# Gathering a unit's attention products into one block on TensorE, beside the MLP's second product

## The chip, the cores and the metric

The kernel runs on one core of a Trainium2 chip. The metric is the device time of one execution in microseconds (us). TensorE is called PE in the profile, VectorE DVE, ScalarE ACT, GpSimd POOL, and SyncE, which issues most DMAs here, SP.

## The reference

Two blocks follow each other. The first is a gated recurrence over 4 batches x 8 heads, 768 tokens, head size 48; the second is an MLP of 384 -> 2048 -> 384 with ELU over the 3072 tokens.

```python
f = 1.0 / (1.0 + np.exp(-f_logit))
state = np.zeros((B, H, D, D), dtype=np.float32)
for t in range(S):
    state = f[:, :, t, :, None] * state + np.einsum('bhd,bhe->bhde', k[:, :, t], v[:, :, t])
    y[:, :, t] = np.einsum('bhd,bhde->bhe', q[:, :, t], state)
# (B,H,S,D) -> (B*S, H*D)
x = np.ascontiguousarray(y.transpose(0, 2, 1, 3)).reshape(B * S, H * D)
h = x @ w_in
g = np.where(h > 0.0, h, np.exp(np.minimum(h, 0.0)) - 1.0)
out = g @ w_out
```

## The kernel before

**Units and steps.** The function `fast` does the work. Tokens are cut into 12 units of 256 tokens (three a batch), and a unit into four chunks of 64 for the recurrence. The MLP's 2048 hidden features are taken in 8 pairs of 256. The main loop (at the end of `fast`) has 12 x 16 steps, T = 0 to 191; unit m has steps 16m to 16m + 15. An even step issues `up(P)`, the first product of one pair of features (L918; for units from 1 on `up7`, L872: ten products of 128x128 tiles, done with seven multiplications in place of eight, "psH" in the profile, L882). An odd step issues `joined(P)` before anything else (L901: three DVE additions and, through `exped`, two ACT activations, L914 and L915) and at its end `down(P - 2)`, the second product of the pair before the last (L950, "psM", L981; seven products), which sums into four PSUM banks m0 to m3 over the unit's eight pairs. So unit m's last `down` is in step 3 of unit m + 1; it also issues the evacuation of the four banks: one ACT copy (L992), five DVE additions (L991) and four stores. Inside `up7`, after the first four products, DVE makes the first addition out of the bank (L891) and `elu` of the pair before (L936), whose sums POOL then makes (L946).

**The order is written by hand.** Instructions go into each engine's queue in the order of the calls. `at_step(T, ...)` puts calls into `plan`; the main loop runs those of step T after `joined` and before `up` or `down`.

**Attention of a unit** is made of these calls, in this order of data:

- `load` (L431): f, k, q, v by DMA on SP into one of two sets of buffers (unit number modulo 2). `gates` (L607): two ACT activations on f.
- `decays(u, p)` for three pairs of heads (L640): a scan and a reciprocal on DVE (L626, L631), products of k and of the q of the pair before on POOL (L621), and after the third a DMA `move` that fills the fourth pair (L633, "f<-f"). `settle` (L655) makes the rest on POOL.
- `transposed` (L662): eight transposes of k on PE into banks a0, a1 ("psT"), copied by ACT.
- `advance` (L718): 64 products of 64x64 tiles into a0, a1 ("psU"), then `step` four times on DVE (L677), which adds up the states.
- `scores` (L694): 64 such products into a0, a1 ("psS"), and `mask`, two DVE products (L713) into the one buffer "at".
- `outputs` (L734): 64 such products into a0, a1 ("psY", L743), and at its end two ACT copies of a few columns into "between" (L750), which stand between these products and the next ones in the same banks.
- `carried` (L752): up to 64 such products onto the same sums ("psY", L763), three ACT copies to xt and two small DMAs. `blend` (L865) prepares xt for the first product on POOL.

From unit 3 on the steps are given by D3 and A3, counted from t = 16 (u - 1), one unit before the unit's own MLP: `load` at t - 16, `gates` at t - 8, `decays` and `settle` at t - 7, -5, -3, -1, `transposed` at t + 2, `advance` at 4, `step` at 5, `scores` at 7, `outputs` at 9, `carried` at 11, `blend` at 13. So the four blocks of 64x64 tiles lie between the MLP's 128x128 products, each alone. `reread` and `check` (L590, L597) read the weights again by DMA and take their smallest and largest values with two DVE reductions (L603), every fourth step from 48 on, the reductions four steps later.

[...]

## Time and profile before

| What | Value |
|---|---|
| Median of 3 runs | 569.24 us (569.01 to 570.13) |
| Span of the profiled execution | 567.3 us |
| Mean granted TensorE clock | 0.997 |
| PE busy, steady units, 256.85 to 388.17 us | 131.32 of 131.32 us |
| DVE, ACT, POOL busy in the same stretch | 97.09, 50.54, 70.11 us |
| DMA share, GB/s in it | 0.33, 88 to 90 |
| One block: psU, psS, psY (L743), psY (L763) | 64 products of 64x64 tiles each |

The page gives the span of one profiled execution, and no other time for it. Its sections are read in this order: busy time of each engine; the span in 40 slices, with the granted clock and the DMA's share; the chain of work that ended last, by engine and line; the costliest groups with their mean duration and the idle time before them. The chain can also be had in order of time, and the timeline shows instructions merged by line: start in us, duration in us, engine, line, operation, tiles written and read, shape, count, and in brackets the idle time before it with what ended it. The ends of matmuls are modelled, so distances of starts are used for TensorE.

DVE's busy tenths in the 40 slices are 8779989785675785885785885786776876745543: 8 or 9 in places up to slice 8, and 5 to 8 after that.

### The profile page before, as it was taken

The page shows a single profiled execution, that of the slowest core. Times are in us where ns is not written, and L with a number is a line of the kernel's source. Part 1 is how long each engine was busy: PE and PEld are TensorE (multiplying, and loading weights), DVE is VectorE, ACT ScalarE, POOL GpSimd, SP SyncE. Part 2 cuts the span into 40 slices and gives each one's busy share as a digit, 9 for nine tenths or more (in the row PEclk, how much of TensorE's full clock was granted, in tenths as well). Part 3 has the DMA queues.
Part 4 walks back from the last instruction along what each step waited for, and adds up shares of the span by engine and source line. Part 5 has one row for each costly group of instructions (what it writes and reads, how often), then busy time and mean ns, then how long its engine had stood idle before and what let it go on. Part 6 is the DMA issues. An engine that isn't in the chain of part 4 may idle for free.

```text
span 567.3 us, 15527 instructions
## 1 busy us (share of the span) xinstructions
PE 547.5 (97%) x6336; PEld 509.7 (90%) x6336; DVE 409.4 (72%) x802; ACT 230.2 (41%) x424; POOL 292.7 (52%) x567
## 2 busy tenths in 40 slices
PE   6879998999999999999999999999999999999996
PEld 3566677999999999999999999999999999999996
DVE  8779989785675785885785885786776876745543
ACT  3287862443343433434343343333343343233331
POOL 6601788475374465456366357257248348325332
PEclk9899999999999999999999999999999999999999
DMA  8997951024024225215216216206206203201001
GB/s 212 266 261 209 298 129 43 3 47 114 3 46 138 65 52 145 79 42 156 78 36 155 86 38 153 86 19 173 84 14 178 84 6 74 84 2 36 29 2 35
DMA packets 38193, 53.30 MB, mean 94 GB/s; under 512 B 3712, under 2 KB 27936, under 8 KB 38112
## 3 DMA queue, kind: packets, MB, share of 16 engines
q1 hardware_dynamic: 37312, 51.62, 34.2%
q8 instruction: 52, 0.85, 0.7%
q10 hardware_dynamic: 800, 0.59, 0.4%
q14 instruction: 29, 0.24, 0.1%
HBM read 44.04 MB, written 4.72 MB: 86 GB/s over the span
## 4 chain that ended last, share of the span: by engine, by line
PE 81%; DMA 7%; DVE 7%; issue 2%; POOL 1%; ACT 1%; SPq 0%; DVEq 0%; ACTq 0%; POOLq 0%
PE psH L882 36%; PE psM L981 36%; DMA area<-in_moe_w_in_dram 4%; PE psS L705 2%; PE psY L743 2%; PE psY L763 2%; PE psU_a L728 2%; DVE f L631 2%; PE psT L669 1%; DMA xt<-xt 1%; DMA f<-f 1%; DVE f L626 1%; DMA k<-in_k_dram 1%; DVE bits L563 1%; DVE area L850 1%
## 5 line engine op out<-in xcount | busy, mean ns | idle before, releaser
L882 PE MATMUL psH<-xt,wi 128*128 128x128 f32 (+1 forms) x1056 | 195.0, 294 | 0.1
L946 POOL TENSOR_TENSOR sums<-gg 128x128 f32<-128x128 f32 x176 | 77.7, 462 | 214.5 <-DVE gg L936 205.9
L882 PEld LDWEIGHTS psH<-xt,wi 128*128 128x128 f32 x1056 | 149.5, 192 | 1.8 <-DVE hh L891 0.4
L914 ACT ACTIVATE gg<-hh 128x512 f32<-128x512 f32 x88 | 55.5, 631 | 232.0 <-DVE hh L904 154.6
L882 PE MATMUL psH<-xt,area 128*128 128x128 f32 x704 | 121.8, 275 | 1.3 <-DVE hh L904 1.0
L882 PEld LDWEIGHTS psH<-xt,area 128*128 128x128 f32 x704 | 106.5, 191 | 6.3 <-PE psH L882 1.3
L891 DVE TENSOR_TENSOR hh<-psH,u 128x256 f32<-128x256 f32 x88 | 37.1, 422 | 93.9 <-ACT u L889 93.9
L981 PE MATMUL psM<-area,sums 128*128 128x192 f32 x528 | 100.2, 326 | 0.0
L981 PEld LDWEIGHTS psM<-area,sums 128*128 128x128 f32 x528 | 88.2, 190 | 0.0
L981 PE MATMUL psM<-wo,gg 128*128 128x192 f32 x352 | 74.9, 335 | 0.0
L631 DVE RECIPROCAL f<-f 128x256 f32<-128x256 f32 x36 | 62.7, 1747 | 1.1
L936 DVE SCALAR_TENSOR_TENSOR gg<-gg,hh 128x512 f32<-128x512 f32 x88 | 61.9, 703 | 1.5 <-ACT gg L915 1.5
L915 ACT ACTIVATE gg<-gg 128x512 f32<-128x512 f32 x96 | 60.6, 631 | 3.0
L981 PEld LDWEIGHTS psM<-wo,gg 128*128 128x128 f32 x352 | 55.2, 190 | 2.0
L904 DVE TENSOR_TENSOR hh<-psH,u43h 128x256 f32<-128x256 f32 (+1 forms) x176 | 54.7, 352 | 3.0
L946 POOL TENSOR_TENSOR sums<-gg,sums 128x128 f32<-128x128 f32 x88 | 47.0, 534 | 6.9
L889 ACT COPY u<-psH 128x128 f32<-128x128 f32 x88 | 23.1, 263 | 60.9 <-PE psH L882 60.9
L621 POOL TENSOR_TENSOR q<-q,f 128x256 f32<-128x256 f32 x48 | 35.7, 745 | 21.8 <-DVE f L631 10.6
L904 DVE TENSOR_TENSOR u43h<-psH,hh 128x256 f32<-128x256 f32 x88 | 37.1, 422 | 12.7 <-PE psH L882 12.4
L621 POOL TENSOR_TENSOR k<-k,f 128x256 f32<-128x256 f32 x48 | 40.7, 851 | 7.1 <-DMA f<-f 5.1
L981 PE MATMUL psM<-area,gg 128*128 128x192 f32 x176 | 43.0, 326 | 0.0
L981 PE MATMUL psM<-wo,sums 128*128 128x192 f32 x176 | 43.0, 326 | 0.0
(97 smaller groups left out, 672.3 us busy)
## 6 DMA issues: line engine op xcount, KB each, us to landing
area<-in_moe_w_out_dram SPq DMA_DIRECT2D x8, 768.0 KB, 9.6
again<-in_moe_w_in_dram SPq DMA_DIRECT2D x16, 384.0 KB, 4.2
again<-in_moe_w_out_dram SPq DMA_DIRECT2D x16, 384.0 KB, 3.5
k<-in_k_dram SPq DMA_DIRECT2D x12, 384.0 KB, 4.5
q<-in_q_dram SPq DMA_DIRECT2D x12, 384.0 KB, 5.4
v<-in_v_dram SPq DMA_DIRECT2D x12, 384.0 KB, 5.8
area<-in_moe_w_in_dram SPq DMA_DIRECT2D x8, 576.0 KB, 8.4
out_dram<-o SPq DMA_DIRECT2D x42, 96.0 KB, 1.7
```

The lines of the kernel that those rows point to most:

```text
L621: e.tensor_tensor(out=t[n][:, p], in0=t[n][:, p], in1=t["f"][:, p, "kq".index(n)], op=ALU.mult)
L631: nc.vector.reciprocal(f[:, p, 1], f[:, p, 0])
L705: nc.tensor.matmul(pc[r][FULL[b], w, p], lhsT=t["k"][FULL[r], p, cols], rhs=t["q"][FULL[r], p, cols], start=True, stop=True,)
L882: nc.tensor.matmul(to, lhsT=lhs, rhs=rhs, start=(n == 0), stop=True, skip_group_check=True)
L889: nc.scalar.copy(u1[:], pa[:, 0])
L891: add = lambda to, x, y: nc.vector.tensor_tensor(out=to, in0=x, in1=y, op=ALU.add)
L904: add = lambda to, x, y: nc.vector.tensor_tensor(out=to, in0=x, in1=y, op=ALU.add)
L914: nc.scalar.activation(g[:], h, AF.Relu, scale=-1.0)
L915: nc.scalar.activation(g[:], g[:], AF.Exp, scale=-1.0)
L936: nc.vector.scalar_tensor_tensor(out=g[:], in0=g[:], scalar=-1.0, in1=phs.pop(P), op0=ALU.add, op1=ALU.max)
L946: nc.gpsimd.tensor_tensor(out=s[:, i], in0=x, in1=y, op=op)
L981: nc.tensor.matmul(pm[bank][:, half * DH : (half + 1) * DH], lhsT=x, rhs=y, start=first, stop=(j == NP - 1), skip_group_check=True,)
```

## The change

Up to unit 4 the attention is still planned call by call (unit 3 in the steps it had; unit 4 now at 29 to 48, earlier by 3 to 8 steps). From unit 5 on, everything comes a unit earlier (t = 16 (u - 2)), and the products are issued together in `turn(u)` at t + 5: `outputs` of unit u - 1, `scores` and `mask` of unit u, `carried` of unit u - 1, `advance` and the four `step` of unit u. Scores go to m3 and m0 and the states' products to m1 and m2, the banks of the second product of unit u - 3, whose last `down` is in step t + 3; outputs and carried keep a0 and a1. The `down` of step t + 5 isn't issued there: step t + 7 issues two, one after the other. So turns are at steps 53, 69, ... 149. Outputs and carried of the last unit stand alone at 165 and 167. `load` is split in two (f and k; q and v), and the rereading of the weights moves by two steps.

```diff
--- before.py
+++ after.py
@@ -401,9 +401,17 @@
     D2 = (16, 18, 20, 22)
     A2 = (23, 25, 25, 26, 27, 28)
     D3 = (-7, -5, -3, -1)
-    A3 = (2, 4, 5, 7, 9, 11)
+    FIRST = 4
+    BEFORE = (
+        (16, 16, 24, (25, 27, 29, 31), (34, 36, 37, 39, 41, 43)),
+        (29, 29, 32, (33, 35, 37, 40), (44, 46, 46, 48)),
+    )
+    SECOND = (40, 43, 42)
+    DS = (-4, -2, 0, 1)
+    TR = 2
+    TURN = 5
     BL = 13
-    RR = 0
+    RR = 2
     MX = 10
     CB = 16
     BL1 = 13
@@ -715,10 +723,10 @@
                 in1=twice[:].unsqueeze(1).broadcast_to([128, NW * HP, C]), op=ALU.mult,
             )
 
-    def advance(u, pairs=range(HP)):
+    def advance(u, pairs=range(HP), banks=("a0", "a1")):
 
         if u not in pus:
-            pus[u] = [ps.tile([128, NW, HP, D], FP32, tag=n, name=f"psU{u}_{n}") for n in ("a0", "a1")]
+            pus[u] = [ps.tile([128, NW, HP, D], FP32, tag=n, name=f"psU{u}_{n}") for n in banks]
         pu = pus[u]
         for p in pairs:
             for w in range(NW):
@@ -829,13 +837,29 @@
         kept = []
         for p, i in enumerate(first):
             at_step(i, (lambda: settle(u)) if p == NKT else lambda p=p: decays(u, p))
+        if not then:
+            return
         if u > 1:
             at_step(then[0], lambda: transposed(u, 0, "a0"), lambda: transposed(u, 1, "a1"))
         at_step(then[1], lambda: advance(u))
         at_step(then[2], *(lambda c=c: step(u, c) for c in range(NC)))
         at_step(then[3], lambda: kept.append(scores(u)), lambda: mask(u, kept[0]))
-        at_step(then[4], lambda: outputs(u))
-        at_step(then[5], lambda: carried(u))
+        if len(then) > 4:
+            at_step(then[4], lambda: outputs(u))
+            at_step(then[5], lambda: carried(u))
+
+    def turn(u):
+
+        if u > FIRST:
+            outputs(u - 1)
+        if u < NU:
+            mask(u, scores(u, ("m3", "m0")))
+        if u > FIRST:
+            carried(u - 1)
+        if u < NU:
+            advance(u, banks=("m1", "m2"))
+            for c in range(NC):
+                step(u, c)
 
     gs, ss, pms, phs = {}, {}, {}, {}
 
@@ -1132,11 +1156,22 @@
     at_step(BL1, lambda: blend(1))
     at_step(30, lambda: blend(2))
     for u in range(3, NU):
-        t = (u - 1) * NFT
-        at_step(t + BL, lambda u=u: blend(u))
-        at_step(t - 16, lambda u=u: load(u))
-        at_step(t - 8, lambda u=u: gates(u))
-        attention(u, [t + i for i in D3], [t + i for i in A3])
+        at_step((u - 1) * NFT + BL, lambda u=u: blend(u))
+        if u <= FIRST:
+            fk, qv, gate, first, then = BEFORE[u - 3]
+            attention(u, first, then)
+        else:
+            t = (u - 2) * NFT
+            fk, qv, gate = (t - 15, t - 10, t - 9) if u > FIRST + 1 else SECOND
+            attention(u, [t + i for i in (D3 if u > FIRST + 1 else DS)], ())
+            at_step(t + TR, lambda u=u: transposed(u, 0, "a0"), lambda u=u: transposed(u, 1, "a1"))
+            at_step(t + TURN, lambda u=u: turn(u))
+        at_step(fk, lambda u=u: load(u, "fk"))
+        at_step(qv, lambda u=u: load(u, "qv"))
+        at_step(gate, lambda u=u: gates(u))
+    at_step((NU - 2) * NFT + TURN, lambda: outputs(NU - 1))
+    at_step((NU - 2) * NFT + TURN + 2, lambda: carried(NU - 1))
+    turns = [(u - 2) * NFT + TURN for u in range(FIRST + 1, NU)]
     for n in range(NR):
         t = 3 * NFT + (NU - 4) * NFT * n // NR + RR
         at_step(t, lambda n=n: reread(n))
@@ -1154,7 +1189,9 @@
             f()
         if T % 2 == 0:
             up(P)
-        elif P >= LAG:
+        elif P >= LAG and T not in turns:
+            if T - 2 in turns:
+                down(P - LAG - 1)
             down(P - LAG)
         for n in later.pop(T, ()):
             split(n)
```

## The prediction

> **What bounds the kernel now.** I read the page first: busy time, chain, costliest groups.

> ```profile
> span 567.3 us, 15527 instructions
> ...
> PE 547.5 (97%) x6336; PEld 509.7 (90%) x6336; DVE 409.4 (72%) x802; ACT 230.2 (41%) x424; POOL 292.7 (52%) x567
> ...
> PE psH L882 36%; PE psM L981 36%; DMA area<-in_moe_w_in_dram 4%; PE psS L705 2%; PE psY L743 2%; PE psY L763 2%; PE psU_a L728 2%; DVE f L631 2%; PE psT L669 1%; DMA xt<-xt 1%; DMA f<-f 1%; DVE f L626 1%; DMA k<-in_k_dram 1%; DVE bits L563 1%; DVE area L850 1%
> ```

> TensorE carries the chain, and the four attention groups are 2% each. A busy PE row alone proves little, so I took the chain in order of time, where each piece starts when the one ahead lets it.

> ```profile
> 322.99 2.44 PE psH L882 x20
> 325.43 1.09 PE psY L743 x64
> 326.52 2.47 PE psM L981 x14
> 328.99 2.44 PE psH L882 x20
> ...
> 335.00 2.44 PE psH L882 x20
> 337.44 2.28 PE psM L981 x14
> 339.71 2.44 PE psH L882 x20
> ```

> Two steps without attention take 339.71 - 335.00 = 4.71 us (I use 4.72 = 2.44 + 2.28). Two steps with one attention block take 328.99 - 322.99 = 6.00 us, so a block costs 1.28 us. A unit has eight such pairs, one set of transposes (8 x 0.11 = 0.87 us) and four blocks: 37.76 + 0.87 + 5.12 = 43.75 us. The timeline has the transposes of neighbouring units at 305.24 and 348.98: 43.74 us. So from about the third unit on TensorE runs without a gap, and a microsecond won or lost there is one of the kernel.

> Now the price of a block's two ends. In the timeline, 64 products of 64x64 tiles start from 325.36 to about 326.31, 15 ns apart: 64 x 15.1 = 0.96 us. The rest of the 1.28 us, 0.32, is the change of tile shape in and out. Next, what ACT does with the outputs block:

> ```profile
> 325.36 1.16 PE L743 MATMUL psY<-at,v 64*64 64x64 f32 x64
> ...
> 326.64 0.63 ACT L914 ACTIVATE gg<-hh 128x512 f32<-128x512 f32 x1 [2.46 <-DVE hh L904]
> 327.30 0.63 ACT L915 ACTIVATE gg<-gg 128x512 f32<-128x512 f32 x1
> 327.84 0.34 ACT L750 COPY between<-psY 128x8 f32<-128x8 f32 x2
> ```

> The small copy "between" (L750) must be done before carried's products may add to the same banks, and stands in ACT's queue behind the step's two activations. It ends 2.8 us after the block began. Here two steps lie between outputs and carried, so nobody waits. Last, the end of a unit, where the change puts its block:

> ```profile
> 311.12 0.30 ACT L992 COPY u<-psM 128x192 f32<-128x192 f32 x1
> ...
> 311.46 0.36 DVE L991 TENSOR_TENSOR o<-psM,u 128x192 f32<-128x192 f32 x1 [1.62 <-ACT u L992]
> 311.92 1.02 DVE L991 TENSOR_TENSOR u<-psM,u 128x192 f32<-128x192 f32 x2
> 312.97 0.82 DVE L991 TENSOR_TENSOR o<-psM,u 128x192 f32<-128x192 f32 x2
> 313.71 1.00 DVE L603 TENSOR_REDUCE spans<-again 128x1 f32<-128x384 f32 x2
> 314.63 0.41 DVE L891 TENSOR_TENSOR hh<-psH,u 128x256 f32<-128x256 f32 x1
> ...
> 316.01 0.62 DVE L904 TENSOR_TENSOR hh<-psH,u43h 128x256 f32<-128x256 f32 x2
> ...
> 316.73 0.63 ACT L914 ACTIVATE gg<-hh 128x512 f32<-128x512 f32 x1 [3.27 <-POOL sums L946]
> ```

> DVE empties the four product banks until 313.79; hh, elu and the joins stand behind that, and the activations behind these.

> [...]

> **The change part by part.** I count from D = 310.83, where the last second-product pair of a unit (start 310.66, pitch 0.16) makes room for the next instruction.

> 1. Fewer changes of shape. Units 4 to 11 have 32 blocks now. After: advance and scores of unit 4 (2), seven turns, outputs and carried of unit 11 (2): 11 runs. 21 x 0.32 = 6.7 us gained, 3 x 0.32 = 0.96 a turn. The products themselves are as many as before.

> 2. The wait in the turn. PE order at step 5 is outputs, scores, carried, advance, and only scores lies between outputs and carried. PE: up of step 4 is done at D + 2.44, outputs start at D + 2.55, outputs and scores take 1.93, so carried is up at D + 4.48. DVE: the evacuation ends at 313.79 = D + 2.96. The checks (L603), which stood next, move by two steps, so hh can start at about D + 2.88 in place of 314.63; from there to the last join the trace shows 316.63 - 314.63 = 2.00, so D + 4.88. ACT: activations 0.1 later, from D + 4.98 and D + 5.64; between starts 0.54 after the second (327.84 - 327.30), D + 6.18, its first copy ends at D + 6.35, carried starts at D + 6.45. The wait is 6.45 - 4.48 = 1.97 us. From below: the step-9 example alone, without the evacuation ahead, gives copy end 2.65 to 2.8 after block start against 1.93, 0.8 us. From above: if hh came only 0.3 us sooner than now, at D + 3.5, 2.6 us. I take 1.97. Net per turn 1.97 - 0.96 = +1.0 us; seven turns +7.1 us. Behind carried on PE stand advance and the next up; DVE's joins and ACT don't wait for these, but PE never gets the time back.

> 3. Banks. Scores needs m3 and m0, released by DVE's first three instructions (by about D + 1.9), before D + 3.5; advance needs m1 and m2, free at D + 2.96. The second product's next group, at step 7, needs mask (0.68 x 2, D + 4.9 to 6.2) and the states (1.84, from about D + 8.6 to 10.5); step 7 comes at about D + 11. Half a microsecond of cover; nothing lost, up to 0.5 a turn if DVE is later.

> 4. The down at step 5 goes to step 7, two in a row: same instructions, 2 x 2.28. Its sums are long done; the rings of gg (4) and sums (3) just suffice: the oldest user of each was read at step 3. Zero. DVE after the turn (states 1.84, check 1.0, hh to join 2.0) ends near D + 13.4; next need is up of step 8 near D + 15.6.

> 5. Loads in two halves, on SP: the same DMAs; q and v wait for carried two units back, at the turn one step earlier. The page gives f 3.6, k 4.5, q 5.4 us to landing; f has six steps (16 us) to its gates, k more, q five (13 us) to its product. The stores and moves that SP queues behind q wait at most for that turn. Zero. For unit 5, f is issued at 40 and used at 42, 6 us for 3.6. Zero, up to 1.

> 6. The packed stretch, steps 29 to 53. Units 4 and 5 make their decays a unit earlier: 3 x (0.75 + 1.75) = 7.5 us of DVE each; between 128 and 184 us the page's slices have DVE at 5, 6, 7 and 5 tenths, so there is room for both on the whole. A late join has about 3.4 us of slack before up needs its bank. One place is short: unit 5's last reciprocal pair is at 48, its settle at 49, its transposes at 50. At 46 DVE has states (1.84, from 1.25 after advance begins) and 2.5 of decays, then 2.0 hh to join, until 7.6; at 48 mask to 8.9, decays to 11.4. POOL then has k, q (0.7 each), sums 1.85, q, k (0.7 + 1.18): to about 16.3. PE reaches the transposes of pair 3 at 12.0 + 0.66. Wait 3.6. The same shape is seen in unit 2, with one step more:

> ```profile
> 97.68 1.17 POOL L621 TENSOR_TENSOR k<-k,f 128x256 f32<-128x256 f32 x1
> ...
> 98.91 0.44 PE L669 MATMUL psT<-ident,k 128*128 128x128 f32 x2 [0.88 <-POOL k L621]
> ```

> There k ends 6.1 us after the reciprocal (92.75), and PE loses 0.9. Bounds 0.5 to 4; I take 3.2, as DVE may win some time.

> Sum: +7.1 + 3.2 = +10.3 us. The profiled span 567.3 becomes 577.6. The page gives no other time for that execution; the span lies 1.9 us under the median, 569.24. I add 1.9: 579.5 us.

> **The rivals.** B, partly hidden: evacuation and joins overlap better than I laid out, the wait in a turn is 0.8 to 1.0 us and eats just what the shape changes give. Then only part 6 is left: 569 to 573, middle 571. For it: the step-9 lines. Against it: the evacuation ahead in the same FIFO. C, the other side: scores covers the copy, because between is done early. The turn then keeps 0.96 x 7 = 6.7, part 6 costs 2, and the time is 564.5 (561 to 568). It decides from a copy that ends at most 1.9 us after the outputs start; the shortest in the trace is 2.8, so it needs a queue order other than the program's. That the change doesn't join the blocks is no other case; it would look like B. D, worse: the gaps bring the clock down. [...] For it: a gap of 2 us after products of small tiles; against it: the granted clock stays at nine tenths or more through the gaps near 95 us.

> **How the numbers follow.** Forecast 0.63 (574 to 584), B 0.15, C 0.08, D 0.14. A measurement of this kernel tells about 0.2%, 1.1 us, from no change. Slower: forecast, D and four fifths of B, 0.88; within: 0.03; faster: C and a bit of B, 0.09. The range drops C and the greater part of D: 569 to 586.

> **What would show it.** Right: in each turn, PE idle of about 2 us ahead of carried's products (L763's successor) with ACT between as releaser, up to seven times; a unit of 44.7 us in place of 43.75; a PE wait of some 3 us on POOL k once, near 180 us; no wait at the second product's first pair. Wrong: carried follows scores at once, units of 42.8 us (C); or scores itself waits on DVE o (D). If units are 43.7 us, B.

## The result, and the profile after

The changed kernel takes 585.46 us (584.74 to 586.2, four runs) against 569.12 us (also four runs by then): ratio 1.030, 95% interval 1.0272 to 1.0329. It is slower by 16.3 us; the forecast was 10.3. Its profiled execution has a span of 584.5 us against 567.3.

Line numbers have moved: first product L906 (was L882), second L1005 (L981), scores L713, advance L736, outputs L751, "between" L758, carried L771. From the page of the changed kernel:

```profile
span 584.5 us, 15570 instructions
...
PE 548.6 (94%) x6336; PEld 513.0 (88%) x6336; DVE 404.0 (69%) x802; ACT 231.5 (40%) x424; POOL 291.5 (50%) x567
...
PE psH L906 33%; PE psM L1005 31%; DVE f L639 3%; PE psY L751 2%; DMA area<-in_moe_w_out_dram 2%; PE psY L771 2%; DVE hh L928 1%; PE psU_m L736 1%; PE psT L677 1%; DMA k<-in_k_dram 1%; DVE u43h L928 1%; ACT gg L938 1%; DMA f<-f 1%; DMA f<-in_f_logit_dram 1%; DVE f L634 1%
```

PE has the same 6336 products and is busy about as long as before, in a span 17 us longer. On balance what came on is waiting; in the busy time fewer shape changes (6.7 us by part 1's estimate) and slower products (three stretches of 3.41 us at half the clock, below) nearly cancel. DVE's join (L928) and ACT's activations (L938) are on the chain now. The chain's pieces in order of time show a turn (start, duration, what):

```profile
235.59 2.44 PE psH L906 x20
238.03 1.16 PE psY L751 x64
...
239.25 0.43 DVE u43h L928
...
239.70 0.63 DVE hh L928 x2
...
240.42 0.64 ACT gg L938
...
241.61 0.16 ACT between L758
...
241.81 1.28 PE psY L771 x61
...
243.16 1.21 PE psU_m L736 x59
244.37 2.64 PE psH L906 x20
247.01 4.55 PE psM L1005 x28
```

It is the path of the forecast, step by step: outputs, and then carried not before join, two activations and the copy. Counted as in the forecast, from D (here 235.43), DVE's hh starts at D + 2.89, the last join ends at D + 4.89 and the copy starts at D + 6.18; the forecast had 2.88, 4.88 and 6.18. The waits table sums it up for PE (total, times, longest):

```profile
PE psY L771 <- ACT between L758: 13.2, 8, 1.9
```

Seven of the eight are the turns; the eighth, 0.7 us, lies in the first 70 us, and the kernel before has it too. In the timeline the gap is 1.73 us in five turns and 1.93 or 1.94 in two. It counts from the modelled end of the last score. From start to start, as the forecast counts, PE stands still for 1.93 to 1.94 us in the five turns and 2.14 in the two; the forecast was 1.97. The two are the turns in which carried belongs to the first unit of a batch: it leaves out the first chunk (240 pairs of weight load and product in the turn in place of 256), so its first products go to the second bank, and wait for the second of the two copies, too.

Distances between the transposes of neighbouring units are 45.14, 44.85, 44.86, 44.85 and 46.40 us, where they were 43.74: three turns cost 1.11 us each, one 1.40, one 2.66. The 0.3 us more in the first of these come from a short stop in advance's products (0.17 us longer than usual from start to start, at 243.35), of a kind that the run with the copy first explains below. In the last one the gap is 1.93 us, as long as in an earlier turn, and half the clock follows. From the windows table (a stretch, its length, busy time and count by engine, then the granted clock):

```profile
241.93:245.34 3.41, 3.41 (x137) 3.26 (x138) 0.05 (x1) 2.09 (x5) 0.00 (x0) 1.00 0.04 8
...
282.89:286.31 3.42, 2.33 (x131) 2.07 (x129) 3.39 (x9) 0.72 (x2) 1.61 (x4) 1.00 0.21 62
286.31:289.72 3.41, 2.56 (x117) 2.51 (x118) 0.71 (x2) 2.16 (x6) 0.12 (x1) 1.00 0.11 34
419.43:422.84 3.41, 1.48 (x88) 1.34 (x83) 1.79 (x4) 1.49 (x5) 1.48 (x4) 1.00 0.21 62
422.84:426.25 3.41, 3.41 (x72) 3.32 (x62) 1.53 (x5) 1.73 (x3) 0.00 (x0) 0.50 0.10 25
```

The trace's clock records show half the clock in this execution for stretches of 3.41 us: from 37.13 (while the kernel starts), 132.71, 183.91 and 422.84 us, and at its very end. The distances of these four are 28, 15 and 70 times 3.413 us, so they lie on one grid of such stretches. The gap ahead of 422.84 lies whole in one stretch of the grid (PE busy for 1.48 of 3.41 us), and the next one has half the clock. The gap of 1.94 us at 285.2 to 287.2 is cut by a boundary of the grid into 1.08 and 0.85, and nothing follows. The clock is 1.00 in the other six turns.

The rest is lost before the first turn, between steps 32 and 52, in three places. Lines from the timeline of the changed kernel; brackets give the idle time before an instruction and what ended it:

```profile
128.12 0.84 ACT L620 ACTIVATE f<-f 128x768 f32<-128x768 f32 x1 [2.67 <-DMA k<-in_k_dram]
...
129.75 0.24 ACT L913 COPY u<-psH 128x128 f32<-128x128 f32 x1
...
130.50 0.49 PE L906 MATMUL psH<-xt,wi 128*128 128x128 f32 x2 [1.09 <-DVE hh L915]
...
132.70 1.48 PE L906 MATMUL psH<-xt,wi 128*128 128x128 f32 x4
...
163.34 0.66 PE L677 MATMUL psT<-ident,k 128*128 128x128 f32 x4 [0.55 <-ACT xt L780]
...
184.04 0.69 PE L677 MATMUL psT<-ident,k 128*128 128x128 f32 x2 [2.67 <-POOL k L629]
```

First, step 32: unit 4's gates stand in ACT's queue and wait 2.67 us for their load. The small copy (L913) that frees the first product's bank stands behind them, DVE's addition behind the copy, and PE waits. Afterwards four products take 1.48 us where 0.82 is usual: the clock is at half. Transposes, up and down of steps 34 and 35 take 2.12 + 4.33 + 3.01 us from start to start in place of 0.87 + 2.44 + 2.28: 3.9 us. Second, step 44: transposes need bank a1, which ACT's copies of carried, issued one step before, still read; with the down ahead, 1.1 us. Third, step 50: pair 3 of unit 5 waits for k, 3.1 us, and the up after it takes 3.78 us, 1.3 too many, for the most part at half the clock. The windows table has the clock, 0.50, in the first and the third:

```profile
132.71:136.12 3.41, 3.41 (x15) 3.23 (x14) 3.21 (x5) 1.81 (x5) 1.69 (x4) 0.50 0.00 0
...
183.91:187.32 3.41, 3.28 (x16) 3.28 (x17) 0.55 (x2) 0.85 (x2) 0.76 (x2) 0.50 0.87 244
```

Sum: 7.4 us in the five turns with a measured distance, about 1.1 each in the first and the last, 3.9 + 1.1 + 4.4 before: 19.0. This execution reached the up of step 30 1.8 us earlier than that of before (118.95 against 120.75), which leaves 17.2, the difference of the spans. These 1.8 us are not the change's: in the runs below the same point lies anywhere from 118.38 to 120.42. The profiled execution is the slowest of the four, with a mean clock of 0.987; the other three have 0.993 to 0.996 and took 0.7 to 1.5 us less. So the sizes of the losses by the clock are those of this execution.

### The profile page after: what moved, and what is told of

It reads as the page before. It is cut to its first block, busy times and chain, and to the rows that moved or that the text cites. A ratio compares the mean times of both kernels' runs of the same rounds, so it can differ in the third digit from the quotient of the medians.

```text
span 584.5 us, 15570 instructions
## 1 busy us (share of the span) xinstructions
PE 548.6 (94%) x6336; PEld 513.0 (88%) x6336; DVE 404.0 (69%) x802; ACT 231.5 (40%) x424; POOL 291.5 (50%) x567
## 3 DMA queue, kind: packets, MB, share of 16 engines
HBM read 44.04 MB, written 4.72 MB: 83 GB/s over the span
## 4 chain that ended last, share of the span: by engine, by line
PE 73%; DVE 11%; DMA 6%; ACT 4%; issue 3%; POOL 2%; SPq 0%; DVEq 0%; ACTq 0%; POOLq 0%
PE psH L906 33%; PE psM L1005 31%; DVE f L639 3%; PE psY L751 2%; DMA area<-in_moe_w_out_dram 2%; PE psY L771 2%; DVE hh L928 1%; PE psU_m L736 1%; PE psT L677 1%; DMA k<-in_k_dram 1%; DVE u43h L928 1%; ACT gg L938 1%; DMA f<-f 1%; DMA f<-in_f_logit_dram 1%; DVE f L634 1%
## 5 line engine op out<-in xcount | busy, mean ns | idle before, releaser
L906 PE MATMUL psH<-xt,wi 128*128 128x128 f32 (+1 forms) x1056 | 197.7, 297 | 1.1 <-DVE hh L915 1.1
L938 ACT ACTIVATE gg<-hh 128x512 f32<-128x512 f32 x88 | 55.5, 630 | 254.5 <-POOL sums L970 123.3
L906 PEld LDWEIGHTS psH<-xt,wi 128*128 128x128 f32 x1056 | 151.5, 194 | 3.2 <-DVE hh L915 1.6
L906 PE MATMUL psH<-xt,area 128*128 128x128 f32 x704 | 123.2, 277 | 1.9 <-DVE hh L928 1.5
L906 PEld LDWEIGHTS psH<-xt,area 128*128 128x128 f32 x704 | 107.8, 194 | 7.3 <-PE psH L906 2.0
L915 DVE TENSOR_TENSOR hh<-psH,u 128x256 f32<-128x256 f32 x88 | 36.4, 414 | 103.8 <-ACT u L913 103.8
L1005 PE MATMUL psM<-area,sums 128*128 128x192 f32 x528 | 100.2, 326 | 0.0
L1005 PEld LDWEIGHTS psM<-area,sums 128*128 128x128 f32 x528 | 88.4, 190 | 0.0
L1005 PE MATMUL psM<-wo,gg 128*128 128x192 f32 x352 | 73.2, 331 | 0.0
L928 DVE TENSOR_TENSOR hh<-psH,u43h 128x256 f32<-128x256 f32 (+1 forms) x176 | 54.7, 352 | 3.0
L1005 PEld LDWEIGHTS psM<-wo,gg 128*128 128x128 f32 x352 | 56.2, 192 | 0.5
L629 POOL TENSOR_TENSOR q<-q,f 128x256 f32<-128x256 f32 x48 | 39.5, 824 | 21.9 <-DVE f L639 9.5
L970 POOL TENSOR_TENSOR sums<-sums,gg 128x128 f32<-128x128 f32 x88 | 47.4, 538 | 0.0
L970 POOL TENSOR_TENSOR sums<-gg,sums 128x128 f32<-128x128 f32 x88 | 42.4, 482 | 6.9
L629 POOL TENSOR_TENSOR k<-k,f 128x256 f32<-128x256 f32 x48 | 39.1, 818 | 11.9 <-DVE f L634 7.6
L1005 PE MATMUL psM<-area,gg 128*128 128x192 f32 x176 | 43.0, 326 | 0.0
L1005 PE MATMUL psM<-wo,sums 128*128 128x192 f32 x176 | 43.0, 326 | 0.0
L928 DVE TENSOR_TENSOR u43h<-psH,hh 128x256 f32<-128x256 f32 x88 | 36.9, 419 | 8.3 <-PE psH L906 8.2
```

What stands on the lines that cost most here:

```text
L629: e.tensor_tensor(out=t[n][:, p], in0=t[n][:, p], in1=t["f"][:, p, "kq".index(n)], op=ALU.mult)
L906: nc.tensor.matmul(to, lhsT=lhs, rhs=rhs, start=(n == 0), stop=True, skip_group_check=True)
L915: add = lambda to, x, y: nc.vector.tensor_tensor(out=to, in0=x, in1=y, op=ALU.add)
L928: add = lambda to, x, y: nc.vector.tensor_tensor(out=to, in0=x, in1=y, op=ALU.add)
L938: nc.scalar.activation(g[:], h, AF.Relu, scale=-1.0)
L970: nc.gpsimd.tensor_tensor(out=s[:, i], in0=x, in1=y, op=op)
```

## The experiments

All times are medians, of four runs where nothing else is said. The kernel before was measured again beside them: 568.06 us (seven runs) with the first four experiments, 568.27 (fifteen) over all. That is 1 us under the 569.12 of the result, and four runs of one kernel lie 1.5 to 4.5 us apart. Between kernels of four runs, differences of 2 us or less are therefore not shown by the times; there the traces decide. The first four experiments change the changed kernel in one place.

**The copy first.**

```diff
     def turn(u):
-        if u > FIRST:
-            outputs(u - 1)
...
     for T in range(NU * NFT):
         P = T // 2
         sevens = order[P][0] >= DIRECT
+        if T in turns:
+            outputs(T // NFT + 1)
         if T % 2 and sevens:
             joined(P)
```

> The changed kernel, but in a turn's step outputs and its two small ACT copies are issued before the step's joins and activations, so that the copy no longer stands behind the two activations in ACT's queue. Theory A (carried waits for that copy): the gap of 1.7 to 1.9 us ahead of carried's products goes, a unit takes 43.0 us (42.8 to 43.3) in place of 44.9, seven turns give 12 to 14 us, the time is 572 (570.5 to 574). Rival B (the long block itself costs, by its small tiles, its banks or its reloads): units stay at 44.7 or more, the time is 583 to 586. Rival C (the wait moves to the next late thing, DVE's states or the join): a new gap of about 1 us in the turn, 578.

580.78 us: 4.7 us better (3.6 if each is compared with the kernel before, measured beside it), not 13. Lines of the timeline of this run, one turn:

```profile
236.88 0.36 ACT L758 COPY between<-psY 128x8 f32<-128x8 f32 x2 [2.39 <-PE psY L751]
...
237.62 1.09 PE L771 MATMUL psY<-q,state 64*64 64x64 f32 x61
...
238.55 0.38 PE L736 MATMUL psU_m<-v,kn 64*64 64x48 f32 x11
...
240.84 1.02 PE L736 MATMUL psU_m<-v,kn 64*64 64x48 f32 x52 [1.91 <-issue]
```

The wait for the copy is gone, as theory A said: carried follows scores at once. A new gap has come, as C said, but not behind the states or the join: "issue" means that the profile shows nothing that PE waited for. It is in all seven turns, 1.03 to 1.91 us, after 158 to 255 pairs, in the advance products in five and in carried in two. Units take 44.1 to 44.3 us, one 44.9. The trace's DMA packets say more. One queue, of the kind that the page calls instruction, has 52 packets of 16,384 bytes. I take it for that of PE, whose 12,672 products and weight loads would then make about 244 a packet, and call such a packet a refill. In every turn a refill lands, and the gap ends soon after that:

```
refill ends (us)  194.77  239.37  283.37  327.19  372.90  416.92  460.89
gap ends          196.38  240.84  284.69  328.65  374.40  418.29  462.37
between             1.61    1.47    1.32    1.46    1.50    1.37    1.48
```

This fits a supply of instructions that falls behind. A pair of weight load and product takes 15 ns here (a block is 32 calls in the code, which the profile shows as 64 pairs). A turn is 256 pairs, 512 instructions, so by that estimate about two refills, in 3.8 us. In six of these turns the next refill starts 3.5 to 4.4 us after the last (285.83 after 282.35, 419.87 after 415.48), the gap included, and in the seventh later.

The same holds in the other runs. Over the changed kernel and all the runs of this document the rows of the turns hold 23 stops of more than 0.1 us that neither a copy nor a fall of the clock explains, and each ends 1.31 to 1.61 us after a refill has landed. The seven waits for the copy in the changed kernel end anywhere from 0.2 to 10 us after one. No run changed the refills alone, so that they are the cause is inferred from this timing and from the rows' lengths below.

**Advance ahead of carried.**

```diff
+        if u < NU:
+            advance(u, banks=("m1", "m2"))
         if u > FIRST:
             carried(u - 1)
         if u < NU:
-            advance(u, banks=("m1", "m2"))
             for c in range(NC):
```

> The changed kernel, but in a turn advance comes ahead of carried: outputs, scores, advance, carried. Theory A: another 0.97 us of products covers the copy, the gap falls from 1.7 to 1.9 us to about 0.8 to 0.9, seven turns give 6.5 us, the time is 579 (577.5 to 580). Rival B (the block's cost isn't the copy): 585.

581.19 us, 4.3 better (3.2 against the kernel before). Where the copy was the last thing to come, the gap was 0.78 to 1.01 us, as theory A said for the added cover of 0.97. But issue gaps of 0.28 to 1.66 us stand in five of seven turns, so the gain is half to two thirds of the one expected.

**f earlier.**

```diff
-        (29, 29, 32, (33, 35, 37, 40), (44, 46, 46, 48)),
+        (27, 29, 32, (33, 35, 37, 40), (44, 46, 46, 48)),
```

> The changed kernel, but f and k of unit 4 are loaded at step 27 in place of 29. Theory A (at step 32 ACT's gates wait 2.7 us for this load, the small copy that frees the first product's bank stands behind them, and PE's gap lowers the clock for some us): the loss at steps 32 to 35 (3.9 us: 1.25 + 0.52 of gaps, 2.1 of lower clock) goes, the time is 581.5 (580.5 to 582.5). Rival (DVE and POOL have too much work in steps 29 to 53, and the next of them is late by as much): at least half comes back by step 44, 583.5 to 585.5.

584.05 us, 1.4 better, which as a time is within the noise (ratio to the kernel before 1.0245 to 1.0309, where the changed kernel has 1.0272 to 1.0329). The trace shows what happened. The first place is healed; ACT's gates no longer wait, and PE goes from transposes to up without a gap:

```profile
129.85 1.04 PE L677 MATMUL psT<-ident,k 128*128 128x128 f32 x8
130.73 0.39 PE L906 MATMUL psH<-xt,wi 128*128 128x128 f32 x2
```

From the up of step 30 to that of step 44 it takes 42.04 us in place of 44.88: 2.8 us won of 3.9. The other 1.1 comes back in steps 38 to 40, where scores and the up stand behind late DVE work. So both theories have a part: the load causes the first loss, and the full DVE takes back about a quarter.

**The transposes later.**

```diff
-            at_step(t + TR, lambda u=u: ...
+            at_step(t + TR + (u == FIRST + 1), lambda u=u: ...
```

> The changed kernel, but unit 5's transposes are issued at step 51 in place of 50, other units' as before. Theory A (they wait 2.7 us for POOL's k, which waits for DVE's reciprocal two steps ahead and stands behind the sums): the 3.1 us of gap and the 1.3 us of lower clock after it go, as an up of 2.44 us and its pair lie between now: 581 (580 to 582). Rival (POOL stays late, and the wait follows to step 51 or to the turn at 53): 583.5 to 585.5.

583.49 us, 2.0 better, again not clear of noise (1.0227 to 1.0294); the profiled execution is the slowest of the four, 586.52. In it the transposes wait no more, but the first turn, two steps on, waits longer:

```profile
183.47 1.21 PE L677 MATMUL psT<-ident,k 128*128 128x128 f32 x8
...
194.07 2.06 PE L771 MATMUL psY<-q,state 64*64 64x64 f32 x62 [2.63 <-ACT between L758]
```

Its gap is 2.63 us in place of 1.73, and carried and advance after it take about 1.7 times as long as usual, at half the clock (194.32 to 197.74). From the up of step 48 to that of step 54 the run needs 21.93 us against 23.43, so 1.5 of 4.4 are won. The rival holds in this trace: the lateness followed. Half the clock also follows the gap of this run's second turn, 1.73 us long, and that unit takes 46.68 us in place of 45.14.

**Shorter rows.** Two kernels keep the change's schedule and take products out of the turn.

```diff
     def turn(u):
-        if u > FIRST:
-            outputs(u - 1)
-        if u < NU:
-            mask(u, scores(u, ("m3", "m0")))
-        if u > FIRST:
-            carried(u - 1)
...
+        carried(u - 1)
+        mask(u, scores(u, ("m3", "m0")))
...
+            at_step(t + TURN - 2, lambda u=u: outputs(u - 1))
             at_step(t + TURN, lambda u=u: turn(u))
```

The second also takes carried out of `turn`, to `t + TURN - 1`.

> The changed kernel, but outputs of unit u - 1 is issued two steps before the turn (step t + 3, before down), and the turn holds carried, scores and advance: 192 pairs of weight load and product in a row in place of 256, one change of shape more a unit (0.32 us). The copy between has two steps of cover. Theory S (with the copy out of the way a long row of 15 ns products outruns the supply of TensorE's instructions; in the run with the copy first the gaps came after 176 to 256 pairs): gaps in some of the turns, 0 to 1.5 us each, at places that differ, units 43.1 to 44.3 us, time 574 to 578. Rival D (a dependency holds the advance products, the banks m1 and m2 or the transposed k): the gap of 1 to 2 us stands ahead of or in advance in every turn, 580 to 583.

> As the run with outputs ahead, but carried also leaves the turn, for step t + 4 before up; the turn holds scores and advance, 128 pairs in a row; two changes of shape more a unit than the joint block. Theory S (supply of instructions): no gap in any turn, units of 43.4 us (37.76 + 0.87 + 4 x 0.96 + 3 x 0.32), time 575.5 (574 to 577), all of the remaining loss before step 53. Rival D (a dependency holds advance): a gap of 1 us or more in each turn, 582 or more.

With 192 pairs (176 in two turns): 576.32 us. Three turns of seven have an issue gap (1.15, 1.19, 0.77 us); four have none, and units without one take 43.02 to 43.19 us. With 128 pairs: 573.79 us, no gap in six of the seven turns, and units of 43.39 us. In the seventh one product, the last but one, comes 0.3 us late, 1.44 us after the end of a refill, and the unit takes 43.69. A turn without a gap, and advance in that seventh:

```profile
238.20 1.16 PE L713 MATMUL psS<-q,k 64*64 64x64 f32 x64
239.18 1.10 PE L736 MATMUL psU_m<-v,kn 64*64 64x48 f32 x64
240.21 0.49 PE L900 MATMUL psH<-xt,wi 128*128 128x128 f32 x2
...
369.34 1.40 PE L736 MATMUL psU_m<-v,kn 64*64 64x48 f32 x64
```

Theory S holds and D falls: the same advance products on the same banks m1 and m2 follow scores at once when fewer instructions stand ahead of them. Also, the forecast's price of a shape change was right: 43.39 is one change less (43.74 - 0.32 = 43.42).

**Outputs ahead, and two of the three places mended.** As the first of the two kernels above (192 pairs), with unit 4's numbers `(27, 29, 32, (33, 35, 37, 40), (45, 46, 46, 48))`.

> As the run with outputs ahead, with f and k of unit 4 loaded at step 27 and its transposes at step 45 in place of 44. Theory A (the loss before step 53 has three places: the gates at 32, the banks of the transposes at 44 held by ACT's copies of xt, POOL's k at 50): the first two go, about 3 + 1 us less than the run with outputs ahead, 570 to 574. Rival: DVE is late all through the stretch and takes it back, within 1 us of that run.

573.52 us, 2.8 better than the run without; the intervals of the two (1.0073 to 1.0124 and 1.0119 to 1.0167) only just meet. The gaps at 34 and 44 are gone, that at step 50 (2.65 us on POOL k) is there still. By the medians most of what theory A gave these two places, 4 us, is found. Four of the seven rows have a stop again (1.42, 1.06, 0.68 and 0.1 us). The kernel is still 1% slower than before.

**One thing of the change, in the old schedule.** From the kernel before:

```diff
-    A3 = (2, 4, 5, 7, 9, 11)
+    A3 = (2, 5, 5, 5, 9, 11)
...
-    RR = 0
+    RR = 2
...
+        if then[1] == then[3]:
+            at_step(then[1], lambda: mask(u, scores(u, ("m3", "m0"))))
         at_step(then[1], lambda: advance(u))
...
+    turns = [(u - 1) * NFT + A3[1] for u in range(3, NU)]
...
-        elif P >= LAG:
+        elif P >= LAG and T not in turns:
+            if T - 2 in turns:
+                down(P - LAG - 1)
             down(P - LAG)
```

> The kernel before, with one thing of the change: scores (into m3 and m0) and advance (into a0 and a1, as before) of a unit are issued together at step t + 5 of its own old schedule, that step's down goes to t + 7, and the rereading is two steps later. Outputs and carried stay alone at t + 9 and t + 11, nothing is moved a unit earlier. One change of shape less a unit, 128 pairs in a row, no copy to wait for, no packed stretch. Theory: units of 43.4 us in place of 43.75, nine units, 2.9 us less than before (2 to 3.2), ratio 0.995. Rival: mask is later than the second product's first pair at t + 7 and gives back 0.3 us or more a unit: ratio 1.000 or above.

566.62 us (ten runs) against 568.27: ratio 0.9964, interval 0.9948 to 0.998. It beats both kernels, if only by 0.4%. Units take 43.37 to 43.39 us, one 44.41: there a row of 128 pairs, too, met a refill (it ends at 398.62, PE goes on at 400.06).

```profile
398.37 0.96 PE L728 MATMUL psU_a<-v,kn 64*64 64x48 f32 x51
400.06 0.44 PE L728 MATMUL psU_a<-v,kn 64*64 64x48 f32 x13 [0.73 <-issue]
```

By the medians the gain is 1.65 us where 2.9 was expected; the interval runs from 1.1 to 3.0. That unit accounts for one of the missing microseconds, and what is left is within the noise.

## Why the prediction was right or wrong

The direction and the mechanism of the turn were right: PE waits in each turn for the copy "between", behind join and activations. Part 2's wait was 1.97 us by the working and 1.93 to 1.94 by the trace, counted alike, in five turns, 2.14 in two; its net per turn +1.0 and 1.11. Part 1's price (0.32 us a shape change) is confirmed by the unit of 43.39 us. Parts 3 and 4 cost nothing, as said: scores and the second product have no wait for banks in the turn.

What failed is the size of the one-time losses, the 3.2 us of part 6 together with the "Zero" of part 5: they measure 9.4, of which some 6 are waits and the rest for the most part slower products at half the clock. The third place, the one named, was right in kind: 3.1 us of wait for 3.2 to 3.6, but with 1.3 of lower clock behind it. The sentence "One place is short" was wrong: there were two more. Part 5 counted steps between a load's issue and its use for units 5 and later, and priced unit 4's load, three steps ahead of its gates, with no line of its own. It is issued only after the move of unit 3 on SP (at 122.87 us; ACT stood idle for it from 125.45), and what waits for it on ACT is not the attention but the copy that PE's next bank hangs on; the run with f earlier shows that. The transposes at 44 were left out: they were moved right behind carried, whose copies read the same two banks.

The time, 585.46, lies 1.5 us above the forecast's 574 to 584, and case D, the lower clock, has a part in that. In this execution half the clock came after one of the seven gaps, 1.6 us, and twice in the packed stretch. Together that is some 5 us of 19, and less in the other three executions, whose mean clock is higher. Against D the forecast had the clock of nine tenths or more through the gaps near 95 us. Those are 0.49 to 0.88 us long in the trace of before; that gaps of some 2 us leave the clock alone was not shown, and half the clock followed one of 1.93 us.

Case C asked for the copy to be done in time and set the time then at 564.5. The run with the copy first made that true and gave 580.78. So C's sum was wrong beyond its condition: no term in it allowed for 256 pairs in a row costing more than four times 64. The stops that it left out are 1.03 to 1.91 us a turn there. In the changed kernel, where carried waits 1.73 to 1.94 us for the copy, six turns have no such stop and one has 0.17 us. So the forecast of its turns was near with this cost left out, and that was luck.

Open: how much idle time in a stretch of the grid it takes for half the clock. In the changed kernel, between 100 and 560 us, it followed the stretches in which PE was idle for 2.54, 1.93 and 1.61 us, and none of the others: of these two have 1.73 us, one 1.61 and the rest 1.14 or less. What sets the moment of a refill is open too. The third place was not removed, only moved.

## What to carry to other kernels

Before putting small operations into one row, ask two things of the row: which small copy stands between its parts, and behind what in its engine's queue (here behind two activations, 1.93 to 2.14 us a turn), and how many instructions a microsecond it needs (here a pair of weight load and product in 15 ns); rows of 64 between longer work were free here, 128 nearly so, 192 about half the time, 240 and more never once the copy was out of the way. Moving work a stage earlier cost 9.4 us here, once, in the stage in which two run together; price each load there by the engine that will wait for it and by what is queued behind that wait. If part of a change pays, try it alone in the old schedule first.

## What the runs showed of the hardware

Rows of 64x64 products at 15 ns a pair stopped after 115 to 255 pairs, with no wait that the profile shows. At 128 pairs 14 of 16 rows have no stop (the other two lose 0.3 and 0.9 us), at 176 or 192 pairs 4 of 7 in one run and 3 of 7 in another, at 240 or 256 with the copy first none of 7. PE went on 1.31 to 1.61 us after the end of a refill; that it stood still for want of instructions is inferred from this. A change of tile shape and back cost 0.32 us by the estimate from the trace of before, and the unit of 43.39 us agrees with it.
